# A convolution by matrix products with a routed expert layer: two chunks of the filter's transform moved ahead, and unit 1's first stage woven into its neighbours

## The chip, the cores and the metric

The kernel runs on one core of a Trainium2 chip. The metric is the device time of one execution in microseconds (us). Three executions of the kernel before took 817.46 us in the median (814.24 to 820.39).

## What is computed

The reference convolves eight sequences of 6336 steps and 128 channels with one filter along the sequence, and then puts a small expert layer on the 128 best rows of each sequence:

```python
Xf = np.fft.rfft(x, n=2 * S, axis=1)        # x: (8, 6336, 128)
Hf = np.fft.rfft(h, n=2 * S, axis=0)        # h: (6336, 128)
y = np.fft.irfft(Xf * Hf[None], n=2 * S, axis=1)[:, :S, :]
scores = np.einsum('bsd,d->bs', y, w_gate)
out = y.copy()
for b in range(8):
    top = np.argpartition(-scores[b], 128)[:128]
    ye = np.maximum(y[b, top] @ w1, 0) @ w2
    out[b, top] += ye / (1 + np.exp(-scores[b, top]))[:, None]
```

## The kernel before, in words

The transforms are done as products with cosine and sine tables on TensorE (PE), all in 32 bit. The length 6400 is split as 50 x 128 (`N1`, `N2`). The work is cut into eight units of one sequence's size (0 to 7); the filter h is handled as unit -1. Each unit passes four stages:

- **a** (line 180): a transform over the 50 points. A unit has 8 blocks (q), each in two halves (t = 0, 1); a half is one group of 16 matmuls, which the trace shows as 32 records since a 32-bit matmul leaves two. Before it a block is folded (`fold`, lines 121 and 122: one sum and one difference of its halves, on DVE or POOL). After it `leave_a` copies the result from PSUM to a large buffer in SBUF (line 197 on ACT, line 195 on DVE). Unit 0's buffer is `big`, that of units -1 and 1 is `reg1`.
- **b** (line 251): a transform over the 128 points in 13 chunks of up to 4 of the 50 rows (the last has 2). The product with h's spectrum is two DVE multiplications per chunk (line 268) and an addition on POOL (line 273).
- **c** (line 286): back over the 128 points, 16 steps per unit, copied out by ACT (line 287) into the buffer `half`. A step of c needs all 13 chunks of b.
- **d** (line 305): back over the 50 points; scores and output.

h itself passes a, and then `stage_h` (line 224) instead of b: 4 matmuls per chunk into two PSUM banks; ACT writes a turned copy (line 229) and scales the bank in place (line 230); `join` (line 237, DVE) adds the two into a buffer `st`, which is written to DRAM for later units and used at once by unit 0. One step "j" of the plan does h's chunk c + 1 and then unit 0's b of chunk c.

The order is written out by hand in a list, `plan`; `merge` deals two lists evenly into one. Every engine runs its own instructions strictly in the order in which the plan's steps issue them, and waits where an operand or buffer isn't ready. So does the queue of SP, which issues nearly all DMAs: an entry that waits holds up those behind it. Before, the plan begins: all of a for h, all of a for unit 0, the 13 steps j, all of a for unit 1; then c of unit 0 dealt with b of unit 1, a of unit 2 with d of unit 0, and so on.

PSUM has two pairs of banks (`pt0`, `pt1`) and four single banks (`pb0` to `pb2`, `pm`). A half block of a takes a pair or two singles; a chunk of b takes a pair; a chunk of h takes two of the four singles. The blocks of x are loaded by `load_x` (line 115), numbered n = 8 (unit + 1) + q; n = 15 is the last of unit 0. The tables for b and h come through `ask` (line 144), six at first.

## Time and profile before

| what | us |
|---|---|
| median of three executions | 817.46 |
| the profiled execution, its own time | 814.97 |
| its span, first to last instruction | 813.2 |
| PE busy | 749.8 |
| DVE busy | 632.6 |
| POOL busy | 553.5 |
| ACT busy | 440.7 |

All numbers below are from this one execution. "Idle" and what ended it are inferred by the profiler from semaphores; "issue" is time in which an engine waited for nothing that the profile shows. PEclk is the clock granted to TensorE: 1.00 is 2.4 GHz, 0.50 is 1.2 GHz. Matmuls are pipelined, so a busy PE is not always one at its peak; the chain of waits gives the pace.

### The profile page before, as it was taken

What the parts mean: (1) busy time and instruction counts of PE and PEld (TensorE: products, weight loads), DVE (VectorE), ACT (ScalarE), POOL (GpSimd) and SP (SyncE); (2) the same over time, 40 slices, a digit from 0 to 9 for tenths busy, and PEclk for the clock granted to TensorE, in tenths of its full rate; (3) what the DMA queues carried; (4) which work ended last, traced back from release to release, by engine and by line L of the source; (5) the groups of instructions that cost most, each with busy time, mean ns of one, the idle gap of its engine ahead of it and who ended that gap; (6) DMA issues with size and microseconds to landing.
All of it is one profiled execution on the core that took longest, in us unless ns stands there. A gap on an engine that the chain in (4) does not pass through costs nothing.

```text
span 813.2 us, 36892 instructions
## 1 busy us (share of the span) xinstructions
PE 749.8 (92%) x16189; PEld 670.2 (82%) x16189; DVE 632.6 (78%) x1092; ACT 440.7 (54%) x897; POOL 553.5 (68%) x408
## 2 busy tenths in 40 slices
PE   6799899999999999999999999999999997788656
PEld 6688788899889988888899889888898887777555
DVE  6469846757675899899768998997779978977882
ACT  5688542465346555666365556554464563464351
POOL 0039929966996599759966897768885657525642
PEclk9899899999999999999999999999999999999987
DMA  8649536567756775678557755698479636603500
GB/s 292 230 158 340 171 115 218 169 200 239 259 166 205 241 247 172 187 230 265 174 168 240 249 184 161 194 330 306 147 210 312 202 98 175 182 11 108 168 11 13
DMA packets 82136, 157.45 MB, mean 194 GB/s; under 512 B 9350, under 2 KB 30072, under 8 KB 81976
## 3 DMA queue, kind: packets, MB, share of 16 engines
q1 hardware_dynamic: 81080, 154.05, 58.6%
q8 instruction: 127, 2.08, 1.0%
q0 software_dynamic: 896, 1.05, 0.4%
q14 instruction: 33, 0.27, 0.1%
HBM read 121.77 MB, written 33.29 MB: 191 GB/s over the span
## 4 chain that ended last, share of the span: by engine, by line
PE 67%; DVE 18%; issue 6%; DMA 4%; ACT 2%; POOL 1%; SPq 1%; POOLq 0%; DVEq 0%; ACTq 0%
PE pb L286 22%; PE pt L251 18%; PE pb L305 11%; PE pt L180 10%; DVE cmp L433 2%; DVE tx L268 2%; PE pb L180 2%; DVE st L309 1%; DVE st L310 1%; PE pb L591 1%; PE pb L224 1%; DVE ss L336 1%; ACT junk L442 1%; DMA out<-st 1%; DMA wbuf<-tab_wb 1%
## 5 line engine op out<-in xcount | busy, mean ns | idle before, releaser
L287 ACT COPY half<-pb 114x512 f32<-114x512 f32 x224 | 147.3, 658 | 181.8 <-PE pb L286 181.2
L319 POOL TENSOR_TENSOR tm<-st,wg 114x1024 f32<-114x1024 f32 (+1 forms) x64 | 151.7, 2371 | 77.2 <-DVE st L310 42.0
L273 POOL TENSOR_TENSOR big<-big,tx 128x512 f32<-128x512 f32 (+1 forms) x104 | 131.4, 1294 | 73.4 <-DVE tx L268 62.2
L273 POOL TENSOR_TENSOR reg<-reg,tx 128x512 f32<-128x512 f32 (+1 forms) x104 | 130.6, 1290 | 48.0 <-DVE tx L268 21.8
L286 PEld LDWEIGHTS pb<-wc,reg 128*50 128x50 f32 x4096 | 119.1, 127 | 8.0 <-issue 5.1
L286 PEld LDWEIGHTS pb<-wc,big 128*50 128x50 f32 x4096 | 116.7, 126 | 10.6 <-issue 9.1
L286 PE MATMUL pb<-wc,reg 128*50 128x64 f32 x4096 | 123.7, 221 | 1.1 <-DVE st L310 1.1
L286 PE MATMUL pb<-wc,big 128*50 128x64 f32 x4096 | 121.0, 220 | 0.0
L305 PE MATMUL pb<-half,wbuf 114*50 114x128 f32 x1792 | 110.1, 273 | 7.7 <-DVE st L310 5.1
L305 PEld LDWEIGHTS pb<-half,wbuf 114*50 114x50 f32 x1792 | 95.7, 122 | 17.6 <-DVE st L310 6.2
L251 PE MATMUL pt<-reg,wbuf 128*128 128x256 f32 x352 | 87.9, 398 | 0.5 <-DVE tx L268 0.5
L251 PE MATMUL pt<-big,wbuf 128*128 128x256 f32 x352 | 88.0, 395 | 0.2 <-DVE ss L336 0.2
L309 DVE TENSOR_TENSOR st<-pb,st 114x512 f32<-114x512 f32 x64 | 44.1, 688 | 52.6 <-PE pb L305 39.3
L251 PEld LDWEIGHTS pt<-big,wbuf 128*128 128x128 f32 x352 | 64.4, 188 | 14.7 <-DVE tx L268 0.5
L268 DVE TENSOR_TENSOR tx<-pt,wbuf 128x1024 f32<-128x1024 f32 (+1 forms) x65 | 76.2, 1173 | 0.0
L251 PEld LDWEIGHTS pt<-reg,wbuf 128*128 128x128 f32 x352 | 63.8, 188 | 14.9 <-DVE tx L268 1.0
L197 ACT COPY reg<-pt 128x800 f32<-128x800 f32 x66 | 58.1, 932 | 33.1 <-PE pt L180 33.1
L268 DVE TENSOR_TENSOR reg<-pt,wbuf 128x1024 f32<-128x1024 f32 (+1 forms) x39 | 45.9, 1177 | 23.3 <-PE pt L251 23.3
L197 ACT COPY big<-pt 128x800 f32<-128x800 f32 x59 | 51.7, 931 | 22.2 <-PE pt L180 22.1
L336 DVE TENSOR_REDUCE ss<-tm 114x16 f32<-114x1024 f32 x48 | 58.3, 1215 | 6.1 <-POOL tm L319 5.5
L180 PE MATMUL pt<-fa,big 50*64 50x100 f32 x2336 | 58.8, 249 | 0.0
L308 ACT COPY st<-pb 114x512 f32<-114x512 f32 x64 | 37.7, 589 | 37.8 <-DMA out<-st 12.5
(167 smaller groups left out, 1183.6 us busy)
## 6 DMA issues: line engine op xcount, KB each, us to landing
wbuf<-tab_at SPq DMA_DIRECT2D x128, 200.0 KB
out<-st SPq DMA_DIRECT2D x128, 200.0 KB
wbuf<-tab_wb SPq DMA_DIRECT2D x84, 256.0 KB
wbuf<-hd SPq DMA_DIRECT2D x84, 256.0 KB
big<-in_x SPq DMA_DIRECT2D x37, 512.0 KB
half<-in_x SPq DMA_DIRECT2D x15, 512.0 KB
hd<-st SPq DMA_DIRECT2D x24, 256.0 KB
reg<-in_x SPq DMA_DIRECT2D x12, 512.0 KB
```

Source lines behind the costliest of these rows:

```text
L180: nc.tensor.matmul(o, w, tab[lanes, c], start=True, stop=True)
L197: nc.scalar.copy(out=o, in_=i)
L251: nc.tensor.matmul(pt[:, k * 256:k * 256 + 256], wt[:, k], rows_of(unit, k0 + k), start=True, stop=True)
L268: v.tensor_tensor(out=dst.rearrange("p h a j k t -> p k h a j t"), in0=src, in1=w, op=ALU.mult)
L273: g.tensor_tensor(out=yv[:, :, r], in0=yv[:, :, r], in1=zv[:, :, 1 - r], op=ALU.add if r else ALU.subtract)
L286: nc.tensor.matmul(pt[i2 * 64:i2 * 64 + N1, o:o + HD], w, wc[:, i2], start=True, stop=True)
L287: nc.scalar.copy(out=hv[0:LN, c * 4 + j:c * 4 + j + 2].rearrange("p j r m t -> p (j r) t m"), in_=pt[0:LN].rearrange("p (j t m) -> p j t m ...
L305: nc.tensor.matmul(pt[r][a * 64:a * 64 + N1, c * 128:c * 128 + 128], ats[c // 2][0:LN, c % 2, a, r], hv[0:LN, :, r, m], start=True, stop=True)
L308: nc.scalar.copy(out=st[:, 512:1024], in_=pt[0][0:LN])
L309: v.tensor_tensor(out=st[:, 0:512], in0=pt[1][0:LN], in1=st[:, 512:1024], op=ALU.add)
L319: e.tensor_tensor(out=tm[:, o:o + z].rearrange("p (a d) -> p a d", d=n), in0=st[:, o:o + z].rearrange("p (a d) -> p a d", d=n), in1=w.unsq ...
L336: v.tensor_reduce(out=ss[u][:, :, :, 4 * i:4 * i + 4].rearrange("p b s c -> p s c b"), in_=tm.rearrange("p (s c b d) -> p s c b d", s=2, c ...
```

## The change

Two chunks of h (0 and 1) are taken out of the steps j and dealt among the last four blocks of a of unit 0; a step j of chunk c then does h's chunk c + 2, and the last two steps have none. Their `join` is issued before the plan's next step. The scaling in place on ACT goes; `join` becomes one DVE instruction that scales and adds, and the matmuls of h write the bank in another order of columns. Blocks 0 and 1 of unit 1's stage a are dealt with the last two steps j and use the four single banks in twos; c steps 4 to 7 of unit 0 are dealt with blocks 4 to 7 of unit 1, and are no longer in the list that is dealt with b of unit 1. In stage a of units 0 and 1 other copies than before go to DVE, unit 1's folds 20 and 22 go from POOL to DVE, and the six tables of `ask(0)` stand in SP's queue after unit 0's first block instead of its fourth. The loads and folds for unit 2 are shifted by a step or two to go with it (that part of the diff is left out).

```diff
+    fringe = [(banks[0], banks[1], None), (banks[2], spare, None)]
+    LEAD = 2
@@ products_a: which PSUM banks a block of stage a uses
-        if unit < 2:
+        if unit < 0 or unit == 0 and q < 4:
             pt = turn(wheel)
+        elif unit == 1 and q < LEAD:
+            pt = turn(fringe)
         else:
             p = pair()
@@ stage_a: which engine copies it out ("s" ACT, "v" DVE)
         engines = "ss"
-        if unit == 1 and q > 2:
-            engines = "sv" if pt[2] is None else "v" if pt[2] is pairs[0] else "s"
+        if pt[2] is None and unit == 0:
+            engines = "sv"
+        elif pt[2] is not None and (unit == 0 and q > 3 or unit == 1) and t:
+            engines = "v"
@@ stage_h
-                nc.tensor.matmul(pt[:, i * 256:i * 256 + 256], wt[:, k + i], rows_of(-1, k0 + k + i),
-                                 start=True, stop=True)
+                nc.tensor.matmul(pt.rearrange("p (a i j t) -> p i a j t", i=2, j=32, t=2)[:, i], wt[:, k + i],
+                                 rows_of(-1, k0 + k + i).rearrange("p (a j) t -> p a j t", a=4), start=True, stop=True)
...
-            nc.scalar.mul(out=pt, in_=pt, mul=cst[:, 2:3])
             got.append(pt)
@@ join (inside stage_h)
-                v.tensor_tensor(out=sv[:, k:k + 2], in0=got[k // 2].rearrange("p (k a d) -> p k a d", a=4, d=HD),
-                                in1=turned[...], op=ALU.add)
+                v.scalar_tensor_tensor(out=sv[:, :, k:k + 2], in0=got[k // 2].rearrange("p (a k d) -> p a k d", a=4, d=HD),
+                                       scalar=cst[:, 2:3], op0=ALU.mult, op1=ALU.add, in1=turned[...])
@@ plan
-    plan = merge(a_list(-1), a_list(0)[:0]) + merge(a_list(0), [])
-    plan += [("j", -1, c) for c in range(len(KCH))] + merge(a_list(1), [])
+    chunks = range(len(KCH))
+    tail = len(KCH) - LEAD
+    plan = merge(a_list(-1), []) + merge(a_list(0)[0:4], [])
+    plan += merge(a_list(0)[4:], [[("h", -1, c)] for c in range(LEAD)])
+    plan += [("j", -1, c) for c in chunks[0:tail]]
+    plan += merge([[("j", -1, c)] for c in chunks[tail:]], a_list(1)[0:LEAD])
+    plan += merge(a_list(1)[LEAD:4], [])
+    early = [("c", 0, c) for c in (4, 5, 6, 7)]
+    plan += merge(a_list(1)[4:], [[s] for s in early])
     for u in range(NU):
         if u + 2 <= NU:
-            both = merge(c_list(u), b_list(u + 1))
+            both = merge(c_list(u)[0 if u else 2:], b_list(u + 1))
@@ folds ("v" DVE, "g" POOL) and when tables are asked for
-            fold(done[0], v if done[0] < 16 or done[0] in (21, 23) else g)
+            fold(done[0], v if done[0] < 16 or done[0] > 19 else g)
...
-                fold_to(min(n + q + 4, 15) if unit < 1 else 23)
+                fold_to(min(n + q + 4, 23 if unit else 15))
...
-            if t and (unit, q) == (0, 3):
+            if t and (unit, q) == (0, 0):
                 ask(0)
@@ the walk over the plan
+        elif kind == "h":
+            joins.append(stage_h(s[2], tabs["j", -1, s[2]][0]))
         elif kind == "j":
...
-            if c == 0:
-                spectra.append(stage_h(0, tabs[s][0])())
-            join = stage_h(c + 1, tabs["j", -1, c + 1][0]) if c + 1 < len(KCH) else None
-            n = KCH[c][1] * HD
-            st = spectra.pop()
+            c += LEAD
+            join = stage_h(c, tabs["j", -1, c][0]) if c < len(KCH) else None
+            n = KCH[s[2]][1] * HD
+            st = spectra.pop(0)
```

SP's queue in the first 40 us. `wc`, `tri`, `wg`, `wgc` are constants; the `in_x` row after them is block 15. Before:

```order
L115 DMA half_76<-in_x 128x1024 x5
L747 DMA wc_78<-tab_wc 128x128
L748 DMA tri_81<-tab_tri 128x2x128
L749 DMA half_76<-tab_tri 114x128
L750 DMA wg_79<-in_moe_w_gate 128x128
L751 DMA wgc_80<-in_moe_w_gate 128x1
L115 DMA half_76<-in_x 128x1024
L144 DMA wbuf_86<-tab_wb 128x512 x6
```

Changed:

```order
L117 DMA half_76<-in_x 128x1024 x5
L146 DMA wbuf_86<-tab_wb 128x512 x6
L759 DMA wc_78<-tab_wc 128x128
L760 DMA tri_81<-tab_tri 128x2x128
L761 DMA half_76<-tab_tri 114x128
L762 DMA wg_79<-in_moe_w_gate 128x128
L763 DMA wgc_80<-in_moe_w_gate 128x1
L117 DMA half_76<-in_x 128x1024
```

Block 15 now stands behind the six tables.

DVE from the fold of block 15 (the last pair of folds) to the first multiplications of unit 0. Before:

```order
L121 TENSOR_TENSOR half_76<-half_76 128x512
L122 TENSOR_TENSOR half_76<-half_76 128x8x64
L237 TENSOR_TENSOR st_722<-pb0_70,half_76 128x2x4x64
L237 TENSOR_TENSOR st_722<-pb1_71,half_76 128x2x4x64
L268 TENSOR_TENSOR big_74<-pt0_68,st_722 128x4x128x2
```

Changed:

```order
L123 TENSOR_TENSOR half_76<-half_76 128x512
L124 TENSOR_TENSOR half_76<-half_76 128x8x64
L199 COPY big_74<-pb1_71 128x2x200
L199 COPY big_74<-pt1_69 128x2x2x200
L242 SCALAR_TENSOR_TENSOR st_616<-pb0_70,cst_82,half_76 128x4x128
L242 SCALAR_TENSOR_TENSOR st_616<-pb1_71,cst_82,half_76 128x4x128
L199 COPY big_74<-pt1_69 128x2x2x200 x2
L242 SCALAR_TENSOR_TENSOR st_697<-pb2_72,cst_82,half_76 128x4x128
L242 SCALAR_TENSOR_TENSOR st_697<-pm_73,cst_82,half_76 128x4x128
L199 COPY big_74<-pt1_69 128x2x2x200
L273 TENSOR_TENSOR big_74<-pt0_68,st_616 128x4x128x2
```

Behind that fold now stand the copies of half blocks (3, t = 1), (4, 1), (5, 1), (6, 1) and (7, 1) of unit 0 and the joins of h's chunks 0 and 1.

DVE from the multiplications of unit 0's chunk 11 to unit 1's copies. Before:

```order
L268 TENSOR_TENSOR big_74<-pt1_69,st_1014 128x4x128x2
L268 TENSOR_TENSOR tx_1030<-pt1_69,st_1014 128x4x128x2
L237 TENSOR_TENSOR st_1035<-pb0_70,half_76 128x2x4x64
L268 TENSOR_TENSOR big_74<-pt0_68,st_1035 128x2x128x2
L268 TENSOR_TENSOR tx_1041<-pt0_68,st_1035 128x2x128x2
L121 TENSOR_TENSOR half_76<-half_76 128x512
L122 TENSOR_TENSOR half_76<-half_76 128x8x64
L121 TENSOR_TENSOR big_74<-big_74 128x512
L122 TENSOR_TENSOR big_74<-big_74 128x8x64
L195 COPY reg1_75<-pb1_71 128x2x200
```

Changed:

```order
L273 TENSOR_TENSOR tx_1007<-pt1_69,st_979 128x4x128x2
L123 TENSOR_TENSOR half_76<-half_76 128x512
L124 TENSOR_TENSOR half_76<-half_76 128x8x64
L273 TENSOR_TENSOR big_74<-pt0_68,st_997 128x2x128x2
L273 TENSOR_TENSOR tx_1052<-pt0_68,st_997 128x2x128x2
L123 TENSOR_TENSOR half_76<-half_76 128x512
L124 TENSOR_TENSOR half_76<-half_76 128x8x64
L123 TENSOR_TENSOR half_76<-half_76 128x512
L124 TENSOR_TENSOR half_76<-half_76 128x8x64
L199 COPY reg1_75<-pt0_68 128x2x2x200
L123 TENSOR_TENSOR big_74<-big_74 128x512
L124 TENSOR_TENSOR big_74<-big_74 128x8x64
```

The last join has gone ahead of chunk 11, fold 20 stands before chunk 12's multiplications, folds 21 and 22 before the copy of half block (2, 1), and fold 23 before that of (3, 1).

## Rows read from the trace of the kernel before

**Rows 1.** Page: busy time per engine; share of the chain by engine.

```profile
PE 749.8 (92%) x16189; PEld 670.2 (82%) x16189; DVE 632.6 (78%) x1092; ACT 440.7 (54%) x897; POOL 553.5 (68%) x408
...
PE 67%; DVE 18%; issue 6%; DMA 4%; ACT 2%; POOL 1%; SPq 1%; POOLq 0%; DVEq 0%; ACTq 0%
```

**Rows 2.** Windows of 10 us: length, busy us (instructions) per engine, PEclk, DMA, GB/s.

```profile
30.00:40.00 10.00, 7.18 (x219) 6.92 (x222) 2.69 (x4) 5.62 (x10) 0.00 (x0) 0.77 0.61 220
...
90.00:100.00 10.00, 7.01 (x176) 6.75 (x180) 9.00 (x9) 3.94 (x7) 9.23 (x8) 0.68 0.40 134
...
100.00:110.00 10.00, 8.55 (x348) 8.03 (x344) 4.72 (x6) 5.97 (x9) 2.83 (x3) 0.98 0.01 3
```

**Rows 3.** Chain in order of time, first 50 us: start, length, what.

```profile
35.64 1.80 issue
```

**Rows 4.** Chain over the whole span, later pieces.

```profile
46.95 1.81 PE pt L251 x8
...
54.25 1.82 PE pt L251 x8
...
57.90 1.83 PE pt L251 x8
...
109.97 3.71 PE pb L286 x128
...
113.69 3.85 PE pt L251 x16
...
163.84 1.53 PE pt L180 x64
```

**Rows 5.** Timeline of the SP queue, 17 to 46 us: start, length, DMA issues.

```profile
28.09 0.36 SPq L115 DMA_DIRECT2D half<-in_x  x1
...
28.50 4.22 SPq L144 DMA_DIRECT2D wbuf<-tab_wb  x6
```

**Rows 6.** Timeline of DVE, 24 to 46 us, idle before in brackets.

```profile
29.92 0.69 DVE L121 TENSOR_TENSOR half<-half 128x512 f32<-128x512 f32 x1 [0.95 <-DMA half<-in_x]
...
34.23 0.69 DVE L121 TENSOR_TENSOR half<-half 128x512 f32<-128x512 f32 x1 [2.82 <-DMA half<-in_x]
...
35.03 0.69 DVE L122 TENSOR_TENSOR half<-half 128x512 f32<-128x512 f32 x1
```

**Rows 7.** Windows of 1 us, PE alone: busy, PEclk, DMA share, GB/s.

```profile
34.00:35.00 1.00, 1.00 (x34) 0.50 1.11 420
...
39.00:40.00 1.00, 1.00 (x33) 0.50 0.00 0
...
41.00:42.00 1.00, 1.00 (x33) 0.50 0.06 16
```

**Rows 8.** Timeline 50 to 60 us, DVE in the j steps.

```profile
53.60 1.22 DVE L268 TENSOR_TENSOR tx<-pt,st 128x1024 f32<-128x1024 f32 x1
...
54.74 1.28 DVE L237 TENSOR_TENSOR st<-pb,half 128x512 f32<-128x512 f32 x2
```

**Rows 9.** Timeline of PE, 84 to 112 us.

```profile
85.48 1.09 PE L224 MATMUL pb<-reg,wbuf 128*128 128x256 f32 x4
...
92.68 1.08 PE L180 MATMUL pb<-fa,half 50*64 50x100 f32 x32 [3.07 <-DVE st L237]
```

**Rows 10.** Timeline of DVE, 82 to 106 us.

```profile
86.01 1.23 DVE L268 TENSOR_TENSOR big<-pt,st 128x1024 f32<-128x1024 f32 x1
...
93.93 1.30 DVE L121 TENSOR_TENSOR half<-half 128x512 f32<-128x512 f32 x1
...
95.27 1.10 DVE L122 TENSOR_TENSOR half<-half 128x512 f32<-128x512 f32 x1
...
104.33 0.99 DVE L195 COPY reg<-pt 128x800 f32<-128x800 f32 x1
```

**Rows 11.** DVE groups by shape: count, busy us, mean ns, idle before.

```profile
L514 DVE SCALAR_TENSOR_TENSOR work<-pm,work 114x256 bf16<-114x256 f32 x6 | 2.3, 419 | 0.1
...
L262 DVE TENSOR_TENSOR tx<-pt,wbuf 128x256 f32<-128x256 f32 x4 | 1.6, 412 | 0.0
```

More of the change, by code (lines that the diff above doesn't have):

```diff
@@ L223, in stage_h @@
             for i in range(2):
-                nc.tensor.matmul(pt[:, i * 256:i * 256 + 256], wt[:, k + i], rows_of(-1, k0 + k + i),
-                                 start=True, stop=True)
-            pv = pt.rearrange("p (a r d) -> p a r d", r=2, d=HD)
-            tv = turned[:, k * 256:k * 256 + 512].rearrange("p (a r d) -> p a r d", r=2, d=HD)
+                nc.tensor.matmul(pt.rearrange("p (a i j t) -> p i a j t", i=2, j=32, t=2)[:, i], wt[:, k + i],
+                                 rows_of(-1, k0 + k + i).rearrange("p (a j) t -> p a j t", a=4), start=True, stop=True)
+            pv = pt.rearrange("p (u r x) -> p u r x", r=2, u=2)
+            tv = turned[:, k * 256:k * 256 + 512].rearrange("p (u r x) -> p u r x", r=2, u=2)
             for r in range(2):
                 nc.scalar.mul(out=tv[:, :, 1 - r], in_=pv[:, :, r], mul=cst[:, 3 + r:4 + r])
-            nc.scalar.mul(out=pt, in_=pt, mul=cst[:, 2:3])
             got.append(pt)
@@ L234, in join @@
             st = wide("st")[:, 0:n]
-            sv = st.rearrange("p (a k d) -> p k a d", a=4, d=HD)
+            sv = st.rearrange("p (a k d) -> p a k d", a=4, d=HD)
             for k in range(0, kn, 2):
-                v.tensor_tensor(out=sv[:, k:k + 2], in0=got[k // 2].rearrange("p (k a d) -> p k a d", a=4, d=HD),
-                                in1=turned[:, k * 256:k * 256 + 512].rearrange("p (k a d) -> p k a d", a=4, d=HD),
-                                op=ALU.add)
+                v.scalar_tensor_tensor(out=sv[:, :, k:k + 2], in0=got[k // 2].rearrange("p (a k d) -> p a k d", a=4, d=HD),
+                                       scalar=cst[:, 2:3], op0=ALU.mult, op1=ALU.add,
+                                       in1=turned[:, k * 256:k * 256 + 512].rearrange("p (a k d) -> p a k d", a=4, d=HD))
             for u in range(2):
@@ L753, in conv_moe @@
     used = 0
-    spectra = []
+    spectra, joins = [], []
     for s in plan:
+        while joins:
+            spectra.append(joins.pop(0)())
         kind, unit = s[0], s[1]
@@ L791, in conv_moe @@
                 v.tensor_scalar(out=lanes16[:, 1:2], in0=cst[:, 0:1], scalar1=-1.0, scalar2=None, op0=ALU.mult)
-            if c == 0:
-                spectra.append(stage_h(0, tabs[s][0])())
-            join = stage_h(c + 1, tabs["j", -1, c + 1][0]) if c + 1 < len(KCH) else None
-            n = KCH[c][1] * HD
-            st = spectra.pop()
-            stage_b(0, c, (tabs.pop(s)[0], [st[:, 0:n], st[:, n:2 * n]]))
+            c += LEAD
+            join = stage_h(c, tabs["j", -1, c][0]) if c < len(KCH) else None
+            n = KCH[s[2]][1] * HD
+            st = spectra.pop(0)
+            stage_b(0, s[2], (tabs.pop(s)[0], [st[:, 0:n], st[:, n:2 * n]]))
             if join:
@@ L815, in conv_moe @@
                 last = unit + 3 == NU
-                for q in ((0,), () if last else (5,), (1,) if last else (6, 1), (4,), (2, 3), (), (), ())[i]:
+                first = ((5,), (6,), (0, 1)) if unit == 0 else ((0,), () if last else (5,), (1,) if last else (6, 1))
+                for q in (first + ((4,), (2, 3), (), (), ()))[i]:
                     load_x(m + q)
-                q = (None, 0, None, None, 1, 4, 2, (3, 5))[i] if last else (None, 0, 5, 6, 1, 4, 2, 3)[i]
+                if last:
+                    q = (None, 0, None, None, 1, 4, 2, (3, 5))[i]
+                else:
+                    q = (None, 0 if unit else 5, 5 if unit else 6, 6 if unit else 0, 1, 4, 2, 3)[i]
                 free = i < 6
```

## The prediction

> **What bounds the kernel now.** I read the page first. PE is busy 92% of the span and holds 67% of the chain that ended last [rows 1]; so only time in which PE waits, or runs at the lower clock, can be won. The windows of 10 us then show where that is in the part that the change touches: PE has 7.18 of 10 us at 30 us, 7.01 at 90 us with a mean PEclk of 0.68, 8.55 at 100 us [rows 2]. Between those places, and after 110 us, it has no gap: in the steps j the chain goes from one b group to the next but one in 3.65 us (54.25 to 57.90), nothing but PE in it, and from 109.97 us on c takes 3.71 us for two steps and b 3.85 us for two chunks [rows 4]. So there are two holes, the end of unit 0's stage a and unit 1's stage a, and the question is what ends each in the new order.
>
> The two levels of the clock show as well: PE had stood idle for 1.80 us at 35.64 [rows 3], and in the three windows from 39 to 42 us it was busy at a granted 0.50, 1.2 GHz instead of 2.4 [rows 7], which cost 1.5 us. A new idle stretch of that size can bring the same again.
>
> The measure: the sum is made against the profiled execution, 814.97 us (span 813.2, 1.8 around it), and carried to the median, which is 2.5 us above. Single runs lie 0.4% to either side of it, so about 1% (8.2 us) can be told from no change.
>
> **Part A: up to the first b of unit 0.** Before, the first b starts at 46.95 [rows 4], right behind h's chunk 0. Now two chunks of h (2 x 1.83 us at the pace of rows 4) lie among the last four blocks. They would be free if PE only filled its gaps. But DVE's order has changed: behind the fold of block 15 now stand the copies of half blocks (3,1) and (4,1), and the second half of h's chunk 0 writes the bank that the first of them empties. So PE stops there until block 15 is loaded, folded and the copy done. Before, the fold only held unit 0's last block, some 6 us later.
>
> Block 15 was issued at 28.09 with the six tables behind it [rows 5], and its fold began at 34.23, released by the DMA [rows 6]. Now the tables go first. From the landing of block 14 (29.92 [rows 6]) the queue has to move six tables of 256 KB, 314 KB of constants and the block's 512 KB, 2.4 MB; at the 420 GB/s of the best window [rows 7] that ends at 35.6, and I take 36.0, as the rate isn't held. Bounds: 34.2 (nothing lost, since the engines had slack) and 38.4 (the whole 4.22 us of issuing the tables [rows 5] added).
>
> Then the fold, 0.80 + 0.69 us [rows 6], and a copy of 0.58 (a little over half of the 0.99 for a pair [rows 10]) put the bank free at 38.1. From there: half a chunk of h 0.9, its two turned copies on ACT and the join until 2.65, the copy of (5,1) 1.0, half block (6,1) 0.77 (half of the 1.53 us that two take [rows 4]), h's chunk 1 1.83, block 7 1.53, h's chunk 2 1.83: 9.6 us. PE will have stood for about 3 us before, so I add 0.8 for the lower clock; a stretch like that before cost 1.5 us or a little more, and half of it falls into these waits. First b at 48.5, **1.55 us later** than before; bounds 45.9 and 51.8 (1.05 earlier, 4.85 later).
>
> **Part B: the steps j.** PE's work per chunk is unchanged, 3.65 us. DVE has two multiplications at a pitch of 1.14 (53.60 to 54.74) and two joins in 1.28 us [rows 8], 3.56 in all, so PE still leads. The join is now one instruction that also scales. For its price the nearest rows are a scalar_tensor_tensor from PSUM with 256 columns, 419 ns, against 412 for a tensor_tensor of the same width [rows 11]: I cost it at nothing. Upper end: 70 ns each for reading the factor from SBUF, 0.05 us a chunk above PE's pace, 0.5 us in all. ACT's scaling goes, but the chain of rows 4 shows PE alone there, so ACT wasn't late. What is won: before, b of chunk 10 ended at 85.48, where the next h group starts [rows 9], 38.5 us after the first b. Now h's short last chunk stands ahead of it: nine periods, 2.74 and 1.83 make 37.4. **1.1 us won**, 0.6 at the low end.
>
> **Part C: from there to the fourth step of c.** Before: 85.48 to 109.97, then four steps at 1.855 [rows 4], 31.9 us. PE waited 3.07 us for the last join before unit 1's first block [rows 9]. Now that join stands ahead of chunk 11's multiplications, and PE has unit 1's blocks 0 and 1 in between. But DVE goes through this list, counted from 85.48: multiplications from +0.5 (86.01 before [rows 10]) to 2.8, join 3.45, chunk 11 to 5.75, fold 20 to 8.15 (1.30 + 1.10 us beside POOL's additions [rows 10], against 0.80 + 0.69 alone), chunk 12 to 9.45, fold 21 to 11.85, fold 22 (alone) to 13.35, and only then the copy of half block (2,1), 0.99 us, to 14.35. With two pairs, half block (3,1) waits for that copy. PE reaches this point at about 11, so it stands for 3 us again. Then (3,1) and (4,0) to 15.9; (4,1) waits for fold 23 and a copy until 16.85 and ends at 17.6; four steps of c and three blocks, all on PE, add 7.4 and 4.6: 29.6. With one stretch of lower clock, taken at 1.7: 31.3. **0.6 us won.** Bounds: 27.8 if the folds run at their speed alone and the clock stays up (4.1 won), 33.0 with two such stretches (1.1 lost).
>
> **Part D: the rest of c with b.** Two groups of c are gone from the merge with seven of b, so four chunks of b come in a row. PE does them in 7.7 us, but each needs a pair that DVE frees in 2.3 us; the fourth ends at about 8.7. **1.0 us lost**, between 0 and 2.5 (if the fourth chunk's tables, which wait for the first chunk's buffers, come late). POOL has two folds less in this stage and keeps up. Everything behind this point has the order of before and is only shifted.
>
> **Sum:** +1.55 - 1.1 - 0.6 + 1.0 = +0.85 us, 815.8 on the profiled execution, **818.3** on the median. Ends of all terms together: -6.2 and +7.9, so 811 to 825.
>
> **A rule to weigh.** The rows of a join's kind show no halving: 256 columns from PSUM and SBUF cost 419 ns in either kind of instruction to within 2% [rows 11]. The Trainium skill (Vector Engine (DVE) Microarchitecture Reference, section "Points that are easy to get wrong") says that this instruction with two non-bf16 sources in SBUF runs at half throughput; here one source is in PSUM, so by its letter it doesn't apply, and by it the joins would take the second rival's time.
>
> **Rivals.**
> 1. *Faster, the holes fill.* If block 15 lands early and DVE's folds keep ahead of the copies, PE never waits: part A at its best bound gives 1.05, part B 1.1, part D takes nothing, and part C shrinks to PE's own work (chunks 11 and 12 of b 2.75, sixteen half blocks 12.25, four steps of c 7.4, so 22.4 and 9.5 won): 11.6 us, **806**. For it: the last join no longer stands between PE and unit 1's blocks. Against it: the list of DVE above, where folds 20 to 22 alone take 6.3 us. Chance 0.13.
> 2. *Slower, the join at half speed.* If a scale-and-add of 512 columns took twice a join's time, 2.56 us a chunk instead of 1.28, DVE would need 4.84 us against PE's 3.65, and ten chunks would cost 12 us: **830**. It decides once a join's pitch exceeds 0.69 us, where DVE passes PE. Against it stand the 419 ns of rows 11. Chance 0.06.
> 3. *Slower by the sum of small waits*, block 15 as late as its bound, two stretches at the lower clock and late tables: 826 and above. Chance 0.05.
> 4. *The change does less than it says:* h's chunks aren't hidden at all but simply moved. That is nearly what part A says, and is in the forecast.
>
> **How the numbers follow.** The forecast, 818.3, has 0.76, with a range of its own of 811 to 825. The range for 8 in 10 takes a bit of the first rival and leaves out the rest: 808 to 825. Faster by over 1% (below 809.3): 0.13; slower by over 1% (above 825.6): 0.11; within 1%: 0.76.
>
> **What would show it.** Part A: the fold of block 15 begins at 35 to 37 us, PE idles before it with the DVE copy as releaser, and the first b starts near 48.5; if it starts before 46, part A is wrong. Part B: the joins' mean, 0.68 us, and a period of 3.65 us. Part C: PE idle for some 3 us behind a DVE copy of unit 1, folds of 1.2 us and more beside POOL; if c's first step starts within 14 us of the end of chunk 10's b, the first rival holds. Part D: a wait of about 1 us among the first four chunks of unit 1's b. A gain or loss behind that stage would contradict the claim that the rest only shifts.

## The result, and the profile after

The changed kernel takes **827.02 us** in the median of four runs (824.64 to 832.45), the kernel before on the same chip 818.92 us: a ratio of 1.0121 with an interval of 1.0076 to 1.0166. The forecast was 818.3 us with a range of 808 to 825, so the change is slower by 1.2% where no measurable difference was forecast. The profiled execution of the changed kernel took 828.94 us (span 827.2), 13.97 us more than that of before. The stages below are read from this one pair of executions and add up to its 14 us; by the ratio the two kernels differ by some 10, so a part of what follows is that pair's own scatter.

The page of the changed kernel, busy time and shares of the chain by engine, beside [rows 1]:

```profile
PE 757.9 (92%) x16189; PEld 675.0 (82%) x16189; DVE 643.9 (78%) x1102; ACT 419.9 (51%) x862; POOL 549.9 (66%) x404
...
PE 64%; DVE 20%; issue 6%; DMA 5%; POOL 2%; ACT 2%; SPq 0%; POOLq 0%; DVEq 0%; ACTq 0%
```

PE is busy for 8 us more with the same 16189 records; as the windows below show, it runs longer at the lower clock. DVE has 11 us more work, ACT 21 us less. The chain's shares hardly move: a loss of 1.7% is read from stages, not from shares. The windows of 10 us, beside [rows 2] (length, busy us and instructions per engine, PEclk, DMA share, GB/s):

```profile
30.00:40.00 10.00, 7.55 (x190) 7.08 (x191) 4.00 (x7) 4.08 (x6) 0.00 (x0) 0.66 0.78 261
40.00:50.00 10.00, 7.70 (x136) 6.27 (x134) 5.17 (x7) 3.19 (x6) 0.00 (x0) 0.66 0.19 72
...
90.00:100.00 10.00, 7.75 (x77) 6.16 (x79) 10.00 (x12) 1.93 (x6) 9.92 (x9) 1.00 0.78 262
100.00:110.00 10.00, 7.24 (x193) 5.91 (x183) 9.90 (x10) 5.15 (x10) 9.71 (x8) 0.83 0.54 175
110.00:120.00 10.00, 8.74 (x226) 8.00 (x228) 4.74 (x5) 2.75 (x4) 3.94 (x3) 0.66 0.01 3
...
130.00:140.00 10.00, 8.38 (x112) 6.64 (x107) 4.32 (x4) 2.34 (x4) 1.80 (x2) 1.00 0.43 141
```

Both holes of before are still there, each now followed by a second window at a mean clock of 0.66, and a third hole has come at 130 us. Between 90 and 110 us DVE has no idle time.

**Up to the first b (part A).** SP's queue, beside [rows 5] (start, length, DMA issues; the second and third lines are the first two of the five loads of constants):

```profile
27.87 3.81 SPq L146 DMA_DIRECT2D wbuf<-tab_wb  x6
31.73 0.74 SPq L759 DMA_DIRECT2D wc<-tab_wc  x1
32.51 1.38 SPq L760 DMA_DIRECT2D tri<-tab_tri  x1
...
36.93 0.45 SPq L117 DMA_DIRECT2D half<-in_x  x1
```

The chain of waits over the same stretch, and on to the first b, beside [rows 3, 4]:

```profile
33.43 1.46 issue
...
36.93 4.10 DMA half<-in_x
...
42.39 0.58 DVE big L199
...
43.01 2.07 PE pb L230 x4
45.08 5.08 PE pt L184 x128
...
55.75 1.82 PE pt L256 x8
```

Block 15 is issued at 36.93 instead of 28.09, lands 4.10 us later, is folded, and DVE copies half block (3,1); only then, at 43.01, may the second half of h's chunk 0 start. DVE and PE tell the same in their timelines, beside [rows 6] (in brackets the idle time before, and what ended it):

```profile
41.05 0.69 DVE L123 TENSOR_TENSOR half<-half 128x512 f32<-128x512 f32 x1 [6.99 <-DMA half<-in_x]
```

```profile
30.98 0.82 PE L184 MATMUL pb<-fa,half 50*64 50x100 f32 x26 [1.61 <-DVE big L199]
...
43.01 2.07 PE L230 MATMUL pb<-reg,wbuf 128*128 128x256 f32 x4 [2.30 <-DVE big L199]
```

Around its idle time PE runs at 1.2 GHz: by its windows of 1 us from 33 to 39 and from 43 to 49 us, where before it was from 33 to 35 and from 39 to 42. PE is busy in these windows for 10.5 us, where before it was 5; the 5.5 us more, at half speed, cost some 2.8 us. The clock fell already in the window of 32 us, while PE was busy, so the pause of 1.46 us at 33.43 lies inside the first stretch; before it PE had stood for 1.61 us, until 30.98. That window and four of the others, beside [rows 7] (length, busy us, PEclk, DMA share, GB/s):

```profile
32.00:33.00 1.00, 1.00 (x44) 0.71 1.04 336
...
34.00:35.00 1.00, 0.11 (x4) 0.50 1.04 393
...
38.00:39.00 1.00, 1.00 (x32) 0.50 0.45 46
...
43.00:44.00 1.00, 0.99 (x2) 0.50 0.07 16
...
48.00:49.00 1.00, 1.00 (x32) 0.50 0.99 377
```

The first b starts at 55.75 instead of 46.95: 8.8 us lost.

**The steps j (part B)** take 39.0 us to the end of chunk 10's b (94.7), against 38.5. The groups of DVE, beside [rows 8, 11] (count, busy us, mean ns, idle before), and the one wait of PE there that cost most:

```profile
L242 DVE SCALAR_TENSOR_TENSOR st<-pb,cst,half 128x512 f32<-128x512 f32 x19 | 13.6, 740 | 2.5 <-ACT half L235 1.5 <-PE pm L230 1.0
...
L519 DVE SCALAR_TENSOR_TENSOR work<-pm,work 114x256 bf16<-114x256 f32 x6 | 2.3, 420 | 0.1
```

```profile
73.10 1.14 PE L230 MATMUL pb<-reg,wbuf 128*128 128x256 f32 x4 [0.91 <-DMA wbuf<-tab_wb]
```

The join takes 740 ns; its predecessor, a plain addition of the same 512 columns, took 681.

**From there to the fourth step of c (part C).** PE and then DVE, beside [rows 9, 10]:

```profile
98.90 1.08 PE L184 MATMUL pb<-fa,half 50*64 50x100 f32 x35 [2.25 <-DVE st L242]
...
110.48 2.58 PE L184 MATMUL pt<-fa,half 50*64 50x100 f32 x64 [2.63 <-DVE reg L199]
113.84 1.61 PE L184 MATMUL pt<-fa,half 50*64 50x100 f32 x32 [0.78 <-DVE reg L199]
115.38 3.11 PE L291 MATMUL pb<-wc,big 128*50 128x64 f32 x64
```

```profile
100.94 1.15 DVE L123 TENSOR_TENSOR half<-half 128x512 f32<-128x512 f32 x1
102.13 1.65 DVE L124 TENSOR_TENSOR half<-half 128x512 f32<-128x512 f32 x1
...
106.63 1.21 DVE L123 TENSOR_TENSOR half<-half 128x512 f32<-128x512 f32 x1
107.88 1.65 DVE L124 TENSOR_TENSOR half<-half 128x512 f32<-128x512 f32 x1
109.45 0.98 DVE L199 COPY reg<-pt 128x800 f32<-128x800 f32 x1
110.35 0.86 DVE L123 TENSOR_TENSOR big<-big 128x512 f32<-128x512 f32 x1
111.24 1.64 DVE L124 TENSOR_TENSOR big<-big 128x512 f32<-128x512 f32 x1
112.80 0.98 DVE L199 COPY reg<-pt 128x800 f32<-128x800 f32 x1
```

DVE works without a pause and PE waits for it three times. Behind the wait of 2.63 us PE runs at 1.2 GHz from 111 us to the middle of the window of 117, busy for some 6 us of that; c's first step takes 3.04 us in the chain instead of 1.93. Before, there was such a stretch too, from 94 to 100 us. One window of it, and then two of the changed kernel:

```profile
95.00:96.00 1.00, 1.00 (x34) 0.50 0.03 4
```

```profile
111.00:112.00 1.00, 1.00 (x33) 0.50 0.06 16
...
116.00:117.00 1.00, 1.00 (x24) 0.50 0.00 0
```
The fourth step ends at 128.80, 34.1 us behind the end of chunk 10's b; before it was 31.9. 2.15 us lost.

**The rest of c with b (part D).** PE, where before it has no wait at all between 112 and 168 us:

```profile
134.28 3.14 PE L256 MATMUL pt<-reg,wbuf 128*128 128x256 f32 x13 [0.95 <-issue]
138.09 2.08 PE L256 MATMUL pt<-reg,wbuf 128*128 128x256 f32 x8 [0.67 <-DVE tx L273]
140.35 2.09 PE L256 MATMUL pt<-reg,wbuf 128*128 128x256 f32 x8 [0.18 <-DVE tx L273]
179.41 0.92 PE L184 MATMUL pt<-fa,big 50*64 50x100 f32 x32 [1.07 <-DVE tx L273]
```

The first four chunks of b take 10.0 us (132.44 to 142.44), and a short last chunk stands alone at the end. 3.4 us lost. Unit 1's c starts at 206.2 instead of 191.3, and the rest of the kernel takes 621 us as before (622).

### The profile page after: what moved, and what is told of

The parts are those of the page before. It is cut to its first block, busy times and chain, and to the rows that moved or that the text cites. A ratio compares the mean times of both kernels' runs of the same rounds, so it can differ in the third digit from the quotient of the medians.

```text
span 827.2 us, 36846 instructions
## 1 busy us (share of the span) xinstructions
PE 757.9 (92%) x16189; PEld 675.0 (82%) x16189; DVE 643.9 (78%) x1102; ACT 419.9 (51%) x862; POOL 549.9 (66%) x404
## 3 DMA queue, kind: packets, MB, share of 16 engines
q0 software_dynamic: 896, 1.05, 0.5%
## 4 chain that ended last, share of the span: by engine, by line
PE 64%; DVE 20%; issue 6%; DMA 5%; POOL 2%; ACT 2%; SPq 0%; POOLq 0%; DVEq 0%; ACTq 0%
PE pb L291 21%; PE pt L256 17%; PE pb L310 10%; PE pt L184 10%; DVE tx L273 3%; DVE cmp L438 2%; POOL tm L324 1%; DVE st L314 1%; DVE st L315 1%; DMA wbuf<-tab_wb 1%; PE pb L596 1%; PE pb L230 1%; DMA out<-st 1%; ACT junk L447 1%; PE pb L184 1%
## 5 line engine op out<-in xcount | busy, mean ns | idle before, releaser
L201 ACT COPY reg<-pt 128x800 f32<-128x800 f32 x65 | 57.2, 931 | 38.4 <-PE pt L184 38.2
L201 ACT COPY big<-pt 128x800 f32<-128x800 f32 x57 | 49.9, 926 | 28.6 <-PE pt L184 28.6
L184 PEld LDWEIGHTS pt<-fa,big 50*64 50x64 f32 x2368 | 52.3, 133 | 7.9 <-issue 4.3
```

Of the source, the lines that this page charges most:

```text
L184: nc.tensor.matmul(o, w, tab[lanes, c], start=True, stop=True)
L201: nc.scalar.copy(out=o, in_=i)
```

## The experiments

Ratios are to the kernel before on the same chip, with 95% intervals; they can differ by up to 0.002 from the quotient of the two medians. The starts (us) are read from PE's timeline of one profile each: the first b, the start of h's last chunk, c's first step of unit 0, and c's first step of unit 1.

| kernel | median us | ratio | b | last h | c | c of unit 1 |
|---|---|---|---|---|---|---|
| before | 815.95 to 818.92 | 1 | 46.8 | 85.5 | 109.9 | 191.1 |
| changed | 827.02 | 1.0121 [1.0076, 1.0166] | 55.6 | 91.9 | 115.4 | 206.1 |
| changed, again | 827.34 | 1.0130 [1.0079, 1.0181] | 52.8 | 88.3 | 111.3 | 201.7 |
| tables back | 824.74 | 1.0090 [1.0057, 1.0122] | 46.5 | 82.8 | 106.2 | 197.1 |
| copies on ACT | 825.83 | 1.0114 [1.0071, 1.0158] | 49.6 | 86.0 | 109.0 | 200.2 |
| folds on POOL | 825.75 | 1.0100 [1.0052, 1.0149] | 51.7 | 87.0 | 109.7 | 202.2 |
| strict merge | 823.13 | 1.0080 [1.0054, 1.0105] | 54.0 | 89.0 | 111.8 | 199.0 |
| c not early | 823.94 | 1.0096 [1.0064, 1.0127] | 51.8 | 87.6 | 115.2 | 196.4 |
| all mended | 819.59 | 1.0043 [1.0015, 1.0071] | 47.3 | 83.8 | 105.7 | 192.5 |
| h ahead only | 820.36 | 1.0021 [0.9989, 1.0053] | 51.2 | 86.8 | 115.3 | 196.6 |
| join alone | 817.29 | 1.0014 [0.9993, 1.0036] | 48.8 | 88.0 | 111.7 | 193.0 |
| h behind | 818.54 | 1.0023 [0.9999, 1.0046] | 48.7 | 84.2 | 114.1 | 195.3 |
| banks | 826.33 | 1.0110 [1.0080, 1.0140] | 54.5 | 89.8 | 113.0 | 203.5 |
| mended, banks | 819.26 | 1.0020 [0.9992, 1.0047] | 51.4 | 87.7 | 106.7 | 193.9 |
| mended, h behind | 817.93 | 1.0015 [0.9994, 1.0037] | 49.6 | 85.9 | 105.6 | 193.6 |
| first half block | 815.56 | 0.9984 [0.9963, 1.0005] | 48.7 | 87.3 | 110.4 | 191.7 |

A single profile scatters: three kernels with the stage a of before have their first b at 46.8, 48.7 and 48.8, and behind unit 1's c the rest takes 620 to 627 us in any of them. So a start is compared within its own stage, and a difference of less than some 2 us between profiles proves nothing. One part of the scatter is in every profile: in the first 40 us PE stands between blocks on nothing that the profile shows, here for 1.46 us at once, 1.54 and 1.80 before, 3.98 in folds on POOL and 4.06 in strict merge. What these stops are stays open. In folds on POOL no wait of PE for the copy behind block 15's fold is left beside its stop, and the first b still starts at 51.7.

**The four places, one at a time.** Tables back: the six tables stand in the queue where they stood before.

```diff
-            if t and (unit, q) == (0, 0):
+            if t and (unit, q) == (0, 3):
                 ask(0)
```

> The changed kernel with one edit: the six tables of ask(0) stand in SP's queue after unit 0's fourth block again, as before the change, so that block 15 goes ahead of them. Theory (block 15 is late because six tables and five constants stand ahead of it in SP's queue, and DVE's copies, PE's banks and so h's chunk 0 wait behind its fold): the fold of block 15 begins at 34 to 37 us instead of 41, PE's wait of 2.3 us before the second half of h's chunk 0 goes or shrinks below 1 us, the first b of unit 0 comes at 47 to 50 us instead of 55.75, and the kernel is 5 to 8 us faster than the changed one, 819 to 822. Rival (the first b is late because PE has two more chunks of h to do there and does them at the lower clock; the block only looks guilty): the first b stays within 2 us of 55, and the time within 2 us of the changed kernel's 827.

Block 15 is issued at 27.73, its fold begins at 34.38 with 2.95 us of idle time before it, and the first b starts at 46.49, where before it started, with both chunks of h in front of it. SP's queue in this kernel:

```profile
25.08 0.42 SPq L759 DMA_DIRECT2D wc<-tab_wc  x1
...
27.73 0.33 SPq L117 DMA_DIRECT2D half<-in_x  x1
28.10 4.25 SPq L146 DMA_DIRECT2D wbuf<-tab_wb  x6
```

The constants take 2.65 us of the queue here (25.08 to 27.73), and 5.20 behind the tables (31.73 to 36.93). Of the 5.20 us the five issues are 3.16; most of the rest SP's queue waits, by the profile, for tables to land. The longest of these waits in the changed kernel (us in total, times, longest):

```profile
SPq L761 <- DMA wbuf<-tab_wb: 1.0, 1, 1.0
```

So part A's loss begins with the place of block 15 in the queue. The time falls by some 3 us only, short of the 5 to 8 expected: DVE's list in part C still holds PE up, here for 3.83 us at once, and a stretch at 0.50 follows it.

```profile
101.33 2.95 PE L184 MATMUL pt<-fa,half 50*64 50x100 f32 x64 [3.83 <-DVE reg L199]
```

Copies on ACT: unit 0's copies are all made by ACT, none by DVE behind a fold; the tables stay first.

```diff
-        if pt[2] is None and unit == 0:
-            engines = "sv"
-        elif pt[2] is not None and (unit == 0 and q > 3 or unit == 1) and t:
+        if pt[2] is not None and unit == 1 and t:
             engines = "v"
```

> The changed kernel with one edit: unit 0's copies out of PSUM are all on ACT, as before the change, so that none stands behind the fold of block 15 on DVE; the tables stay ahead of the block. Theory (late block and DVE's order together make the loss): the fold still begins near 41 us, but PE does blocks 4 to 6 and both chunks of h before it without a wait for a DVE copy, and only block 7 waits; the first b at 46 to 48 us, 819 to 821. Rival (the late block alone costs it, through block 7, whoever copies): the first b stays after 52 us and the time above 824. Rival (PE's own work at the lower clock): the first b within 2 us of 55.

The fold of block 15 still begins late, at 38.77, but the first b starts at 49.55 and no wait of PE for a DVE copy is left there; so the late block costs that much because the copies stand behind its fold: in the changed kernel's second profile (below) the fold begins at 38.65, as here, and the first b at 52.82. The other 3 us stay, so this is neither the 46 to 48 of the theory nor the 52 of the rival, and in the time it can't be told from the changed kernel.

Strict merge: the list of c and b is dealt group by group (two chunks of b, two steps of c), beginning with b, and the short last chunk goes with the group before it.

```diff
-            both = merge(c_list(u)[0 if u else 2:], b_list(u + 1))
+            if u:
+                both = merge(c_list(u), b_list(u + 1))
+            else:
+                bs = b_list(1)
+                both = merge(bs[:-2] + [bs[-2] + bs[-1]], c_list(0)[2:])
```

> The changed kernel with one edit: in the stage of unit 0's remaining c steps and unit 1's b, two chunks of b and two steps of c alternate strictly, b first and c last, with b's short last chunk beside the two ahead of it, instead of two c steps, four chunks of b in a row and the short chunk at the very end. Theory (the merge of 6 with 7 makes PE wait for pairs: 10.0 us for four chunks instead of 7.7, and 1.07 us at the end): the four-chunk wait and the one at the end go, 2 to 3.5 us faster than the changed kernel, 823.5 to 825. Rival (POOL's additions and folds set that stage's pace): the waits move to later chunks, and the time is within 1 us of 827.

From the end of c's fourth step to unit 0's first d it takes 48.7 us instead of 51.4, and of the four waits of part D one of 0.64 us is left. The time falls by 3.5 to 4 us, about what the theory expected, though the intervals overlap.

Folds on POOL: folds 20 and 22 go back to POOL.

```diff
-            fold(done[0], v if done[0] < 16 or done[0] > 19 else g)
+            fold(done[0], v if done[0] < 16 or done[0] in (21, 23) else g)
```

> The changed kernel with one edit: folds 20 and 22 of unit 1 are on POOL again, 21 and 23 on DVE, as before the change. Theory (DVE's list between chunk 11's multiplications and the first copies of unit 1 makes PE stand before half block (3, 1), where it waited 2.63 us in the changed kernel): DVE's copy of half block (2, 1) comes about 5 us sooner, that wait goes, and the kernel is 2 to 3 us faster, 824 to 825. Rival (POOL's additions for chunk 12 now come behind fold 20 and hold c's first step): the wait moves to c's first step, and the time is within 1 us of 827 or above it.

From the start of h's last chunk to c's first step it takes 22.7 us instead of 23.5, which proves nothing, as the five other profiles with the folds of the change and c early have 22.8 to 23.5. The time is 1 to 2 us less than that of the changed kernel, which the intervals don't tell from nothing. PE's four waits there got shorter in sum (2.19, 0.55, 0.40 and 1.54 us against 2.25, 0.61, 2.63 and 0.78).

The changed kernel was run again beside the next ones.

> The changed kernel itself, timed beside the others on one chip, since the first comparison rests on few executions. Theory: 6 to 10 us slower than the kernel before (ratio 1.008 to 1.012); in its profile the fold of block 15 begins at 38 to 42 us and the first b of unit 0 comes at 51 to 56 us. If the first b comes before 49 us here, the late block of the first profile was one execution's chance.

Its ratio is the same to 0.1%, and so are the reasons: block 15 issued at 34.20, landed 4.42 us later, fold at 38.65, first b at 52.82. Part A's loss varies by 3 us from run to run.

c not early: c's steps 4 to 7 go back into the list dealt with b of unit 1, and the loads and folds for unit 2 to their old places (that part of the edit is left out).

```diff
-    early = [("c", 0, c) for c in (4, 5, 6, 7)]
-    plan += merge(a_list(1)[4:], [[s] for s in early])
+    plan += merge(a_list(1)[4:], [])
...
-            both = merge(c_list(u)[0 if u else 2:], b_list(u + 1))
+            both = merge(c_list(u), b_list(u + 1))
```

> The changed kernel without its early steps of c: the steps 4 to 7 of unit 0 are back in the list that is dealt with unit 1's b, and the loads and folds for unit 2 as before the change. Theory (the early steps cost: DVE's folds of unit 1 and POOL's early folds for unit 2 slow each other, and six groups of c with seven of b make PE wait 3.4 us): unit 1's folds on DVE take less, the four chunks of b no longer come in a row, and the kernel is 3 to 5 us faster than the changed one. Rival (the early steps do fill holes of unit 1's stage a, as they were meant to): without them the time is the changed kernel's or longer.

Some 3 us are gained, as with the strict merge, and it mends the same place another way: between c's first step and d there is no wait of PE at all.

**All four together** (tables back, copies on ACT, folds on POOL, strict merge):

> The changed kernel with four edits together: tables behind unit 0's fourth block, unit 0's copies on ACT, folds 20 and 22 on POOL, strict alternation of c and b. Theory (the losses stand in these four places and add): first b of unit 0 at 45 to 49 us, no wait above 1 us among the first chunks of unit 1's b, and a time 8 to 11 us below the changed kernel's, between 2 us faster and 1 us slower than the kernel before. Rival (what is won early is given back later in the kernel, so that single mends of 7 us show as 2): still 4 us or more slower than the kernel before.

819.59 us, some 7 less than the changed kernel by the ratios, with intervals that don't overlap. So these four places hold most of the loss. It is less than the 8 to 11 us expected, and the kernel is still slower than the one before, by 0.4%. What is left of the change is h ahead, the new join, unit 1's first blocks among the last steps j and the early c, and that wins nothing.

**h ahead only** is that kernel with c not early in place of the strict merge:

> The changed kernel with the tables behind unit 0's fourth block, unit 0's copies on ACT, folds 20 and 22 on POOL, and without the early steps of c: what is left of the change is h two chunks ahead, the join as one instruction, and unit 1's blocks 0 and 1 among the last two steps j. Theory (h ahead and the two blocks fill holes, the rest of the change loses): first b at 45 to 48 us, unit 1's stage a done 1 to 4 us sooner than in the kernel before, and as fast or up to 4 us faster than it. Rival (h ahead gains nothing, since DVE and the clock set the pace at both holes): within 1.5 us of the kernel before or slower.

It can't be told from the kernel before. PE had waited 4.45 us for h's first table here, and run at 0.50 behind that wait, and the first b came at 51.2. This is the other side of the tables' old place: behind block 15 they come late for h's chunk 0, which now stands among the blocks. PE waits for that table in three of the four profiles with both (4.45 us here, 4.39 in mended, banks, 0.96 in all mended, none in tables back).

**Join alone** is the kernel before with the one-instruction join and the matmuls' order of columns that goes with it:

> This is the kernel before with one thing of the change alone: h's matmuls write the other order of columns, ACT's scaling is gone, and the join is one instruction that scales and adds; the plan, the tables and the folds are those of before. Theory (the loss lies in the new order of work, not in the new instruction): the two joins of a chunk take 1.36 to 1.4 us instead of 1.28, DVE then needs about 3.6 us a chunk beside PE's 3.65, so the steps j keep their pace to within 0.5 us and the time is 0 to 1 us above that of before, a ratio of 1.000 to 1.001. Rival (the new instruction is what costs, by DVE passing PE's pace in twelve of the thirteen steps, or by the new column order slowing PE's writes): 4 us and more above before, a ratio of 1.005 and more, and a period of the steps j of 3.9 us or longer.

1.0014: as the theory expected, within the interval of no difference. The joins take 742 ns and the steps j from the first b to h's last chunk 39.25 us instead of 38.7.

**h behind** is the h-ahead-only kernel with the two chunks behind unit 0's last block:

```diff
-    plan += merge(a_list(0)[4:], [[("h", -1, c)] for c in range(LEAD)])
+    plan += merge(a_list(0)[4:], []) + [("h", -1, c) for c in range(LEAD)]
```

> This is the kernel of the run with h ahead only (tables in the old place, unit 0's copies on ACT, folds 20 and 22 on POOL, c not early), with h's chunks 0 and 1 put behind unit 0's last block instead of among its last four. Theory (h's chunks among the blocks cost something, since PE there waits for h's table and for the banks, and runs at 0.50 behind the wait; there are no holes that they could fill): PE has no wait for a table behind block 3, the first b begins at 48.5 to 49 instead of 51.2 us (before's 46.95 and the 1.83 us of a second chunk), which the join of chunk 1 and the last steps then give back, and the time is 1 to 2.5 us less, a ratio to the kernel before of 0.996 to 1.001. Rival (the chunks do fill gaps, and the late first b of that run was its own chance): the first b at 50 us or later, and a time equal or up to 2 us more, a ratio of 1.002 to 1.005.

The wait for the table is gone and the first b starts at 48.70, both as the theory has it, but the ratio of 1.0023 lies above its range and in the rival's, and is that of h ahead only (1.0021) over again. Putting h's chunks among the blocks neither costs nor wins what can be measured.

**Banks, in the changed and in the mended kernel.** PE's wait of 2.25 us before unit 1's first half block is for the last join, since that half takes the two banks the last chunk of h used. One line gives it the other two:

```diff
-    fringe = [(banks[0], banks[1], None), (banks[2], spare, None)]
+    fringe = [(banks[2], spare, None), (banks[0], banks[1], None)]
```

> This is the changed kernel with the two pairs of single banks for unit 1's blocks 0 and 1 in the other order: block 0 takes the banks that h's chunk 11 has left, block 1 those of chunk 12, the last one. Both theories expect PE's wait of 2.25 us for the last join before block 0 to go. Theory (DVE sets the pace there: from 84 to 114 us it has no idle time, and its order of work is the same in both kernels): the time comes back as a longer wait for the copies behind folds 21 to 23, c's first step starts 0 to 0.7 us earlier counted from the end of chunk 10's b, and the ratio to the kernel before stays at 1.011 to 1.014. Rival (the wait itself is what stage C lost): 2 to 3 us less, c's first step 18 us behind the end of chunk 10's b instead of 20.7, and a ratio of 1.008 to 1.010.

> This is the kernel with all four mends (tables in the old place, unit 0's copies on ACT, folds 20 and 22 on POOL, the strict merge) and with those two pairs of banks in the other order too. There DVE stood idle for 2.99 us before chunk 12's multiplications, because PE came late to that chunk after its 2.19 us wait for the last join and a stretch at 0.50. Theory: block 0 starts at once behind chunk 11's b, DVE's idle time and the low clock after it go, c's first step comes 2 to 4 us earlier than 22 us behind the start of h's last chunk, and the ratio to the kernel before falls from 1.0043 to 0.999 to 1.002. Rival (the folds beside POOL bound this place as well): c's first step less than 1 us earlier, and a ratio of 1.003 to 1.006.

In the changed kernel the ratio stays at 1.011, and from h's last chunk to c's first step it takes 23.2 us instead of 23.5: the wait cost nothing that shows, as DVE has no idle time there and sets the pace. The first half block starts at once, and the wait comes back as others: PE's waits in that stretch are 1.25, 1.79, 2.80 and 0.42 us, 6.26 in all, against 6.27 with the old order. The two longest:

```profile
102.69 2.65 PE L184 MATMUL pt<-fa,half 50*64 50x100 f32 x64 [1.79 <-DVE tx L273]
...
108.14 2.94 PE L184 MATMUL pt<-fa,half 50*64 50x100 f32 x64 [2.80 <-DVE reg L199]
```

In the mended kernel, where DVE had 2.99 us of idle time, the same edit shortens that stretch from 21.9 to 18.9 us (19.7 in the next run, which has it too). Its ratio fell to 1.0020, at the edge of what the theory expected and not to be told from 1.0043. In that profile PE waited for h's first table once more:

```profile
38.39 3.75 PE L228 MATMUL pb<-reg,wbuf 128*128 128x256 f32 x8 [4.39 <-DMA wbuf<-tab_wb]
```

**What is left.** The mended kernel with the banks in the other order and h's chunks behind the last block:

> This is the kernel with the four mends and the other order of the two pairs of single banks, and with h's chunks 0 and 1 put behind unit 0's last block instead of among its last four. Theory (the rest of the loss is PE's wait for h's first table, 4.39 us in the run before, and the low clock behind it): no such wait, the first b at 48.5 to 49.5 us, c's first step 19 us behind the start of h's last chunk as in the run before, and a ratio to the kernel before of 0.997 to 1.000. Rival (the rest lies elsewhere, spread over the stages behind): the same first b, but a ratio of 1.001 to 1.004.

The wait is gone and the first b starts at 49.57. The ratio, 1.0015, lies in the rival's range, but its interval reaches into the theory's.

The last one is the kernel before, with only the first half block of unit 1 in two banks that h's last chunk doesn't use:

```diff
-        if unit < 2:
+        if unit == 1 and (q, t) == (0, 0):
+            pt = (banks[2], spare, None)
+        elif unit < 2:
             pt = turn(wheel)
```

> This is the kernel before with one edit: unit 1's very first half block goes to the two single banks that h's last chunk doesn't use, and the rotation of banks goes on from there, so every later half block of unit 1 has the banks of its predecessor. Before, PE waited 3.07 us for the last join ahead of that half block. Theory (DVE's list sets the pace there): the first half block starts some 3 us earlier, but the next ones wait for the last join and for chunk 12's multiplications as before, c's first step comes 0.5 to 2 us earlier, and the ratio is 0.997 to 1.000. Rival (the wait itself is what the place costs): c's first step 3 us earlier and more, and a ratio of 0.994 to 0.997.

The half block starts at once, the next one waits 2.15 us for the join, and c's first step comes 23.1 instead of 24.4 us behind the start of h's last chunk (23.7 in join alone, which has the old banks). 0.9984 is what the theory expected, and it is the lowest median of all, yet its interval reaches 1: no version was shown to beat the kernel before.

## Why the prediction was wrong, point by point

- **The frame held.** PE's waits and its low clock are where the time moved, the four parts named hold the loss, and behind them the order only shifts (621 against 622 us).
- **Part A failed, by its size.** The forecast was 1.55 us, between 1.05 won and 4.85 lost; 8.8 us were measured, and 6.0 in the second profile. The mechanism was as described: PE stands until block 15 is loaded and folded and the copy of (3,1) made. The step that failed is "six tables of 256 KB, 314 KB of constants and the block's 512 KB, 2.4 MB; at the 420 GB/s of the best window [rows 7] that ends at 35.6, and I take 36.0". It counted bytes and took the queue for free. The block landed at 41.03 instead of 36.0: the tables' issues took 3.81 us, the constants then 5.20 instead of 2.3, partly in waits for tables to land, and the block's landing another 4.10. The bound of 38.4 added only the tables' issues. From the bank's release the path to the first b was 12.8 us, 2.4 more than worked out: from 43 to 49.5 us half blocks and a half chunk of h ran at 1.2 GHz, which cost some 3.2 us, where 0.8 had been set.
- **Part B failed by its sign:** 0.5 us lost, not 1.1 won. The join's price was within its bounds (60 ns more, against an upper end of 70), but two joins and two multiplications now take 3.58 us of DVE against PE's 3.65, so there is hardly any slack: PE waited 0.91 us for a late table, and 0.21 us for a join behind the casts before chunk 6, which cost DVE 0.86 us before too and held up nobody. The other 0.5 us are in no single row.
- **Part C failed by its size:** 2.15 us lost, with 0.6 won forecast and 1.1 lost as the end. "Fold 22 (alone)" was one step, half of the miss: POOL had early folds for unit 2 there (107.25 to 114), and it took 2.82 us from start to start instead of 1.34. The four folds 20 to 23 took 9.8 us of DVE, against 5.4 alone. By that the copy of (2,1) ended 15.7 us behind chunk 10's b instead of 14.35. The other half of the miss is the lower clock: the stretch behind PE's wait cost some 3 us, where 1.7 had been taken, though the trace of before has one of over 6 us in the same place (PEclk 0.68 over 10 us, [rows 2]). PE's wait for the last join, which the forecast had dissolved, stayed at 2.25 us; that one cost nothing that shows, by the run with other banks.
- **Part D failed by its size:** 1.0 us was set, 3.4 measured. The four chunks in a row cost 2.3, the bound of 2.5 for them held; overlooked was that a list of seven dealt into six leaves the short last chunk alone at the end.
- **The rivals.** The holes didn't fill. The join at half speed didn't come: 742 ns against 681 for the same columns. So the Trainium skill's halving for this instruction (Vector Engine (DVE) Microarchitecture Reference, section "Points that are easy to get wrong"), which is stated for two non-bf16 sources in SBUF, did not appear with one in PSUM. The third rival, the sum of small waits at 826 us and more, is what happened, with the block as late as its bound and later, more stretches at the low clock and a late table. It had been given 0.05. The fourth, that h's chunks are only moved, fits h among the blocks (1.0021) against h behind them (1.0023). The terms were sized each from its likely value, and all four missed to the same side. A likely reason, which no run tests, is that each came from a schedule in which only the named wait was late.

Not settled is the last 1 to 2 us between the mended kernels and the one before, which only the interval of the first of them (1.0015 to 1.0071) separates from nothing, nor why single mends are worth less in the time than in their stage: where a wait went, a later one grew.

## What to carry to other kernels

Before moving loads in a queue, add the issue times of all that now stands ahead, and not at the lowest price seen (0.42 us an issue here, with up to 1.38 behind the tables, and waits between them), and follow who is queued behind the consumer: here one fold held up a copy, a bank, and with it PE. A wait on PE is priced with the clock behind it: two such stretches were set at 0.8 and 1.7 us and cost some 3 each. A wait is worth something only if the engine that ends it has idle time; the same one-line edit won 3 us in its stretch where DVE had some, and nothing where it had none, though neither showed in the time. Where two engines are within 2% of each other's pace, as DVE and PE in the steps j, a late operand isn't made up for.

## What the runs showed of the hardware

- An issue of a DMA on SP took 0.42 us (`tri`, line 760) with the tables behind it, and 1.38 us behind six tables, with the DMA engines at a share of 1.04 in the window of 32 us. The same five issues took 2.65 and 5.20 us, waits between them included. The tables alone don't explain a long issue: that of `tri` took 1.37 us in h ahead only and 1.90 in mended, h behind, where they stand behind it.
- A fold half of 512 columns, two sources in SBUF, took 0.69 us on DVE alone and 0.86 to 1.65 us beside POOL's work, while a multiplication with one source in PSUM took 1.21 to 1.23 us in both. This fits the Trainium skill (SBUF — State Buffer, section "SBUF: two separate sides"), by which, of a DVE operation with two SBUF inputs and a GpSimd one that reads SBUF, the first to start holds the shared ports for its whole instruction.
- Around two stands of PE it was granted 0.50, 1.2 GHz, for some 6 us each time. From 33 to 39 us it was behind a stand of 1.61 us and over one of 1.46 that lay inside, from 43 to 49 us behind one of 2.30. Before, behind 1.80 us, it had been 3 us. The price of a wait on PE is not the wait alone.
